# Linear attention and a gated MLP on one core: five chunks of 115 tokens for k^T v, other steps for the extra weight cuts, fetches ahead of stores

## The chip, the core and the metric

The kernel runs on one core of a Trainium2 chip. The metric is the device time of one execution in microseconds; the time before is 957.9 us, the median of five executions (956.86 to 958.39). Engines are called as the profile calls them: PE is TensorE (matmuls; PEld are its weight loads), DVE is VectorE, ACT is ScalarE, POOL is GpSimd, SP is SyncE, which here issues nearly all DMAs.

## What is computed

```python
# q, k, v: float32 [8 batches, 8 heads, 576 tokens, 64]
kv  = einsum('bhsd,bhse->bhde', k, v)          # 64 x 64 per head
o   = einsum('bhsd,bhde->bhse', q, kv)
x   = o / sqrt(mean(o*o, -1) + 1e-6) * g_norm  # 576 x 64 per head
x   = x laid out as (8*576 tokens, 8*64)
h   = x @ w_in                                 # w_in  512 x 2048
g   = h * erf(softplus(h))
out = g @ w_out                                # w_out 2048 x 512
```

The weights come as float64 and are seen by the kernel as pairs of int32, from which it builds float32.

## The kernel before

**Tiling.** Tokens are worked in groups of 512 (`G`), four per partition (`J`). A group T = 0 to 7 is the first 512 tokens of batch T; a ninth group gathers the last 64 tokens of all batches (`x_last`). Heads go in pairs (`NP` = 4 pairs), so that one pair fills 128 partitions. For a pair, `attention` returns six pieces: `products` (k^T v into PSUM, its two 64 x 64 blocks copied into the block-diagonal `bd_kv`, and q transposed), `apply` (q times `bd_kv`), `halve`, `mean`, `norm` (the RMS norm; L330 to L369) and `split`, which writes the three rounded forms of x (`x_forms`, L387 on ACT, then L390 and L393 on DVE).

k^T v sums over the tokens of a batch, 576 of them. The tile of k holds 96 rows (partitions) with six tokens each per head (`KR`, `C`); six matmuls per head, one for each token of a row, add up in PSUM (L281). A pair takes 12 matmuls; each is fp32 and shows as two in the profile. The loads of q, k and v are made in `load_pair`: k and v in one DMA each (L130). A pair's loads are issued two pairs ahead, in `products_and_loads`.

**Stages.** The run has three.

- Stage T=0 (to about 155 us): the weights are loaded raw (`w_raw`, four buffers, L182 and L187), converted on DVE and ACT (`w_split` L197 and L206, `w_join`), and group 0 is multiplied in plain fp32 (`h_ps` L671, `o_ps` L502). SP issues, in order: the first pairs' loads, then raw weights, with the loads of the first two pairs of T=1 between them.
- Stage T=1 (about 150 to 262 us), 16 steps f = 0 to 15: the hidden products go over to three products of rounded forms (L444: `n_ps` two thirds, `m_ps` one third), and the weights are cut into their three parts on the way. `to_cut[f]` lists the tiles cut in step f: `w_upper` makes the first part on ACT (L411), `w_lower` the other two on DVE one step later (L414, L417), and the parts are stored to DRAM (`w_kept`). A tile cut in a buffer of `w_in_p` (four buffers) is stored by one DMA of 768 KB (L484). An extra tile of w_out is cut in place, in columns of `w_in_sb` that are no longer needed, and stored by three DMAs of 256 KB (L480); `places_w` says in which step and in which of three places. In a step, the first two entries of `w_new` get their `w_lower` at the start, a third one after the gates (L697).
- The steady part (262 to 951 us), 28 batches of four hidden blocks, m = 8 to 35, and one more for the last results. A batch does four hidden products (weights from `w_in_parts`), with pieces of the attention of group T+1 between them, and then four results of the batch before (weights from `w_out_parts`), whose sums are added to `e` on DVE (L422 for the first sum, L427 for the second). The order of the instructions on every engine is the order of the program.

**Queues of the steady part.** `places` says behind which of the nine places of a batch (0 ahead of all, 1 to 4 after a hidden product, 5 to 8 after a result) each piece of attention goes; as a rule (0, 2, 3, 5, 6, 8). `FETCH` says which weight parts are fetched at each place; `w_in_p` has four buffers and `w_out_p` seven, and a fetch waits on SP until its buffer is free. In the last batch of a group the four tiles of `e` are stored (L513), each in `result`, that is before the fetch of its place. SP works its queue in order.

These lines carry the steps that the change touches:

```python
for j in range(J):
    result(T2, b2, j, g, w)        # in the last batch of a group: store(T, j, es.pop(j))
    fetch(BATCH + j)
    ...
    pieces(BATCH + 1 + j)
```

Of the kernel before, what the change touches and what calls it, by code (L numbers as in the profile page):

```python
# [39 lines left out]
FP32 = mybir.dt.float32  # L40
# [10 lines left out]
BATCH = 4  # L51
# [9 lines left out]
def kernel(  # L61
# [18 lines left out]
    KC = DM // P  # L80
    FC = DF // P
    NG = B + 1
    KR = 96
    C = S // KR
    assert D == 64 and R == 64 and B == 2 * J and DM == H * D and KC == NP and C * KR == S

    const = ctx.enter_context(tc.tile_pool(name="const", bufs=1))
    kvp = ctx.enter_context(tc.tile_pool(name="kvp", bufs=2))
# [26 lines left out]

    q_last = const.tile([P, 2, 2, D], FP32, name="q_last")

    def load_pair(i):
        T, p = divmod(i, NP)
        if T >= B:  # L120
            return
        pool = early if i in (2, 3) else kvp
        side = nc.scalar if i < 3 else nc.sync
        t = q_sb[T, p] = pool.tile([P, J, 2, D], FP32, name="q_sb", tag="q")
        nc.sync.dma_start(
            out=t, in_=q[T, 2 * p : 2 * p + 2, 0:G, :].rearrange("h (p j) d -> p j h d", j=J)
        )
        for name, got, src in (("k", k_sb, k), ("v", v_sb, v)):
            t = got[T, p] = pool.tile([KR, 2, C, D], FP32, name=f"{name}_sb", tag=name)
            side.dma_start(  # L130
                out=t.rearrange("r h c d -> r h (c d)"),
                in_=src[T, 2 * p : 2 * p + 2].rearrange("h (r c) d -> r h (c d)", c=C),
            )

    def load_last(T, p):
        if T < B:
# [118 lines left out]
    def attention(T, p, pools=None):  # L255

        st = {}

        halves = FIRST <= T < B
        bd = bd_kv[:, (T * NP + p) % 2, :]  # L260

        q_tail, o_tail = slice(P, 2 * P), slice(2 * P, 2 * P + R)

        def bank(name):
            pool, tag = (pools or {}).get(name, (ps_at, "at"))
            return pool.tile([P, G], FP32, name=name, tag=tag)

        def square_tile(name):

            if T == 0:  # L270
                return gate.tile([P, G], FP32, name=name, tag="h")
            return attp.tile([P, G], FP32, name=name, tag="qT")

        def products():

            kv_ps = st["kv"] = bank("kv_ps")
            ks, vs, qs = (x.pop((T, p)) for x in (k_sb, v_sb, q_sb))
            for c in range(C):
                for i in range(2):
                    s = slice(i * D, i * D + D)  # L280
                    nc.tensor.matmul(  # L281
                        kv_ps[s, s],
                        lhsT=ks[:, i, c],
                        rhs=vs[:, i, c],
                        start=(c == 0),
                        stop=(c == C - 1),
                    )
            if p % 2 == 0:
                nc.tensor.transpose(kv_ps[:, q_tail], q_last[:, p // 2], ident)
            if p == NP - 2:  # L290
                for i in range(NP):
                    load_last(T + 1, i)
            st["qT"] = square_tile("qT")
            for i in range(2):
                s = slice(i * D, i * D + D)
                nc.vector.tensor_copy(out=bd[s, s], in_=kv_ps[s, s])
            if p % 2 == 0:
                tails[T] = attp.tile([P, P], FP32, name="qT_last", tag="t")
                nc.vector.tensor_copy(out=tails[T], in_=kv_ps[:, q_tail])
            st["tail"] = tails[T][:, p % 2 * R : p % 2 * R + R]  # L300
            qt_ps = bank("qt_ps")
            for j in range(J):
                nc.tensor.transpose(qt_ps[:, j * P : j * P + P], qs[:, j], ident)  # L303
            nc.scalar.copy(st["qT"], qt_ps)

        def apply():
            qT, o_ps, kv_ps = st["qT"], bank("se_ps"), st.pop("kv")
            nc.tensor.matmul(kv_ps[:, o_tail], lhsT=bd, rhs=st.pop("tail"), start=True, stop=True)
            nc.tensor.matmul(o_ps, lhsT=bd, rhs=qT, start=True, stop=True)  # L309
            nc.vector.tensor_copy(out=x_last[:, p, T * R : T * R + R], in_=kv_ps[:, o_tail])  # L310
            st["o"] = o_ps
            nc.scalar.activation(qT, o_ps, AF.Square)

        def square():
            st["o"], st["qT"] = x_last[:, p, :], square_tile("sq")
            nc.scalar.activation(st["qT"], st["o"], AF.Square)

        def halve():
            sq = st.pop("qT")
            hi = st["hi"] = attp.tile([P, G], FP32R, name="sq_hi", tag="rms_r")  # L320
            lo = st["lo"] = attp.tile([P, G], FP32R, name="sq_lo", tag="sq_lo")
            nc.vector.tensor_copy(out=hi, in_=sq)
            nc.vector.tensor_tensor(out=lo, in0=sq, in1=hi.bitcast(FP32), op=ALU.subtract)

        def mean(table=True):
            ms = st["ms"] = bank("ms_ps")
            if halves:


                nc.tensor.matmul(ms, lhsT=mean_w, rhs=st.pop("hi"), start=True, stop=False)  # L330
                nc.tensor.matmul(ms, lhsT=mean_w, rhs=st.pop("lo"), start=False, stop=True)
                u = square_tile("u")
            else:
                u = st.pop("qT")
                nc.tensor.matmul(ms, lhsT=mean_w.bitcast(FP32), rhs=u, start=True, stop=True)
            if T > 0:
                r = attp.tile([P, G], FP32, name="rms_r", tag="rms_r")
                exp_ln_table()
            else:
                r = gate.tile([P, G], FP32, name="rms_r", tag="s")  # L340
            st["u"], st["r"] = u, r
            nc.scalar.activation(r, ms, AF.Ln, bias=eps_col)  # L342
            nc.scalar.activation(r, r, AF.Exp, scale=-0.5)  # L343
            nc.scalar.activation(u, r, AF.Square)
            if table and (T > 0 or p == NP - 1):
                softplus_table()

        def norm():
            ms, u, r = (st.pop(name) for name in ("ms", "u", "r"))
            nc.vector.scalar_tensor_tensor(  # L350
                out=u, in0=ms, scalar=EPS, in1=u, op0=ALU.add, op1=ALU.mult
            )
            nc.vector.scalar_tensor_tensor(
                out=u, in0=u, scalar=3.0, in1=r, op0=ALU.subtract, op1=ALU.mult
            )
            if T < FIRST:
                if T not in xT:
                    xT[T] = wide.tile([P, KC, G], FP32, name="xT", tag="h")
                x = xT[T][:, p, :]
            else:  # L360
                x = st["x"] = x_new.tile([P, G], FP32, name="x", tag="x")
            nc.vector.scalar_tensor_tensor(
                out=x,
                in0=st.pop("o"),
                scalar=gm_col,
                in1=u,
                op0=ALU.mult,
                op1=ALU.mult,
            )  # L369

        def split():
            if T >= FIRST:
                thirds(st.pop("x"), *(form[:, p] for form in x_forms[T]))

        def products_and_loads():
            products()
            load_pair(T * NP + p + 2)

        if T == 0:
            return products, apply, halve, mean, norm  # L380
        first = (products_and_loads, apply) if T < B else (lambda: None, square)
        return (*first, halve if halves else lambda: None, mean, norm, split)
# [218 lines left out]

    others = [("in", f) for f in range(WHOLE)]
    others += [("out", f) for f in (*range(FC - BATCH, FC), *range(FC - BATCH))]
    places_w = {3: 0, 5: 1, 6: 0, 8: 1, 9: 2, 10: 0}
    to_cut = {f: [] for f in range(FC)}
    for f in range(BATCH * (NB - 1)):
        to_cut[f] = [("in", f + WHOLE), others.pop(0)]
        if f in places_w:
            to_cut[f].append((*others.pop(0), places_w[f]))
    to_cut[FC - BATCH] = [("in", FC - 2), ("in", FC - 1)]  # L610
    assert not others
    hs, ss, plain = {}, {}, {}
    whole = FIRST * FC - BATCH
# [131 lines left out]
    def result(T, b, j, g, w):  # L745
# [12 lines left out]
        else:  # L758
            add_scaled(es[j], ps[0], SHIFT - 1.0)
        add(es[j], ps[1])  # L760
        if b == NB - 1:
            store(T, j, es.pop(j))


    FETCH = ("", "in", "in", "out", "in", "out", "in", "out out")
# [2 lines left out]
    for m in range(first_batch, batches + 1):  # L768
# [15 lines left out]
        if T + 1 == B:  # L784
            places = (0, 0, 0, 5, 6, 7)
            if b == NB - 1:

                places, todo[3] = (0, 0, 0, 4, 5, 6), partial(todo[3], table=False)
        elif T + 2 == B and b == NB - 1:
            places = (0, 2, 3, 5, 6, 7)  # L790

        def pieces(place):
# [34 lines left out]
        for j in range(J):  # L827
            result(T2, b2, j, g, w)
            fetch(BATCH + j)
            if j == 1 and m == batches - 1:  # L830
                cut_lower(h, 0, g_next[0])

# [41 lines left out]
```

## Time and profile before

| | us or share |
|---|---|
| median of five executions | 957.9 |
| profiled execution, its own time | 956.94 |
| its span | 955.1 |
| PE busy | 932.7 (98%) |
| DVE busy | 740.6 (78%) |
| ACT busy | 616.2 (65%) |
| DMA queue q1, share of 16 engines | 75.9% |
| granted clock of PE | 1.0 |

The profile is of one execution; the time that is not in its span, 1.84 us, lies around it. Busy times are sums over instructions. The page also lists the costliest groups of instructions with what they waited for, and the DMA issues with the median time from issue to landing; other views list the waits of an engine, the chain that ended last, the instructions in order of time, and the busy time in windows.

### The profile page before, as it was taken

The page shows a single profiled execution, that of the slowest core. Times are in us where ns is not written, and L with a number is a line of the kernel's source. Part 1 is how long each engine was busy: PE and PEld are TensorE (multiplying, and loading weights), DVE is VectorE, ACT ScalarE, POOL GpSimd, SP SyncE. Part 2 cuts the span into 40 slices and gives each one's busy share as a digit, 9 for nine tenths or more (in the row PEclk, how much of TensorE's full clock was granted, in tenths as well). Part 3 has the DMA queues.
Part 4 walks back from the last instruction along what each step waited for, and adds up shares of the span by engine and source line. Part 5 has one row for each costly group of instructions (what it writes and reads, how often), then busy time and mean ns, then how long its engine had stood idle before and what let it go on. Part 6 is the DMA issues. An engine that isn't in the chain of part 4 may idle for free.

```text
span 955.1 us, 11913 instructions
## 1 busy us (share of the span) xinstructions
PE 932.7 (98%) x4384; PEld 686.3 (72%) x4384; DVE 740.6 (78%) x1054; ACT 616.2 (65%) x825; POOL 2.4 (0%) x10
## 2 busy tenths in 40 slices
PE   6999999999999999999999999999999999999998
PEld 4444445556587887888788878887888787878886
DVE  3979957778577887778888887887777777778667
ACT  3889875677666666666666666666666666665552
POOL 0000000000000000000000000000000000000000
PEclk9999999999999999999999999999999999999999
DMA  9856506799599886998689877988796769767972
GB/s 273 268 162 214 163 1 234 274 342 323 210 360 377 310 301 220 312 380 284 221 280 371 311 286 232 358 310 286 225 364 255 265 222 370 281 261 271 365 277 63
DMA packets 110107, 259.80 MB, mean 272 GB/s; under 512 B 44256, under 2 KB 67808, under 8 KB 110048
## 3 DMA queue, kind: packets, MB, share of 16 engines
q1 hardware_dynamic: 108416, 256.73, 75.9%
q10 hardware_dynamic: 1568, 2.29, 0.8%
q8 instruction: 35, 0.57, 0.2%
q14 instruction: 24, 0.20, 0.1%
q0 software_dynamic: 64, 0.00, 0.0%
HBM read 224.40 MB, written 34.60 MB: 271 GB/s over the span
## 4 chain that ended last, share of the span: by engine, by line
PE 69%; DVE 13%; ACT 12%; issue 3%; DMA 2%; SPq 0%; DVEq 0%
PE n_ps L444 36%; PE m_ps L444 18%; PE o_ps L502 5%; PE h_ps L671 3%; PE se_ps L309 3%; PE kv_ps L281 2%; DVE h L427 2%; ACT L105 1%; PE qt_ps L303 1%; ACT s L818 1%; ACT s L822 1%; DVE e L427 1%; DVE g_forms L390 1%; ACT rms_r L342 1%; ACT rms_r L343 1%
## 5 line engine op out<-in xcount | busy, mean ns | idle before, releaser
L444 PE MATMUL n_ps<-x_forms,w_in_parts 128*128 128x512 f32 x896 | 234.0, 402 | 1.3 <-DVE x_forms L390 1.2
L444 PE MATMUL n_ps<-w_out_parts,g_forms 128*128 128x512 f32 x928 | 231.6, 391 | 0.6 <-DMA w_out_parts<-w_out 0.6
L444 PEld LDWEIGHTS n_ps<-w_out_parts,g_forms 128*128 128x128 f32 x928 | 174.2, 188 | 39.3 <-issue 1.4
L444 PEld LDWEIGHTS n_ps<-x_forms,w_in_parts 128*128 128x128 f32 x896 | 166.7, 188 | 46.3 <-issue 9.6
L818 ACT ACTIVATE s<-h 128x512 f32<-128x512 f32 x112 | 71.0, 634 | 177.9 <-DVE h L427 177.9
L427 DVE TENSOR_TENSOR h<-m_ps,h 128x512 f32<-128x512 f32 x116 | 79.9, 689 | 61.5 <-ACT h L816 43.7
L444 PE MATMUL m_ps<-w_out_parts,g_forms 128*128 128x512 f32 x464 | 124.2, 389 | 0.0
L444 PE MATMUL m_ps<-x_forms,w_in_parts 128*128 128x512 f32 x448 | 120.1, 390 | 0.0
L502 PE MATMUL o_ps<-w_out_sb,h_sb 128*128 128x512 f32 x224 | 100.8, 593 | 0.3 <-DVE h_sb L622 0.3
L444 PEld LDWEIGHTS m_ps<-w_out_parts,g_forms 128*128 128x128 f32 x464 | 87.1, 188 | 18.1
L444 PEld LDWEIGHTS m_ps<-x_forms,w_in_parts 128*128 128x128 f32 x448 | 84.1, 188 | 17.5
L427 DVE TENSOR_TENSOR e<-m_ps,e 128x512 f32<-128x512 f32 x116 | 80.3, 692 | 17.9 <-PE m_ps L444 10.4
L422 DVE SCALAR_TENSOR_TENSOR e<-n_ps,e 128x512 f32<-128x512 f32 x88 | 60.3, 686 | 41.6 <-PE n_ps L444 41.6
L502 PEld LDWEIGHTS o_ps<-w_out_sb,h_sb 128*128 128x128 f32 x224 | 42.3, 190 | 48.9 <-issue 46.7
L393 DVE SCALAR_TENSOR_TENSOR g_forms<-g_forms 128x1024 fp32r<-128x1024 f32 x58 | 71.1, 1226 | 2.0
L390 DVE TENSOR_TENSOR g_forms<-h,g_forms 128x1024 fp32r<-128x1024 f32 x58 | 70.6, 1218 | 1.7 <-ACT g_forms L387 1.4
L816 ACT ACTIVATE h<-n_ps 128x512 f32<-128x512 f32 x112 | 65.6, 586 | 8.2 <-PE se_ps L309 4.3
L387 ACT ACTIVATE g_forms<-h 128x1024 fp32r<-128x1024 f32 x58 | 58.9, 1060 | 12.4 <-PE m_ps L444 9.8
L834 DVE TENSOR_TENSOR h<-h,s 128x1024 f32<-128x1024 f32 x56 | 66.0, 1219 | 0.7 <-ACT s L822 0.7
L671 PE MATMUL h_ps<-xT,w_in_sb 128*128 128x512 f32 x144 | 64.9, 594 | 0.8 <-DVE w_in_sb L230 0.6
L108 ACT ACT_TABLE_LOAD x44 | 56.5, 1283 | 0.7
L822 ACT ACTIVATE s<-s 128x1024 f32<-128x1024 f32 x56 | 56.2, 1052 | 0.3
(98 smaller groups left out, 1021.2 us busy)
## 6 DMA issues: line engine op xcount, KB each, us to landing
w_out_parts<-w_out SPq DMA_DIRECT2D x116, 768.0 KB, 8.0
w_in_parts<-w_in SPq DMA_DIRECT2D x112, 768.0 KB, 6.7
w_in<-w_new SPq DMA_DIRECT2D x16, 768.0 KB, 4.8
k_sb<-in_k_dram SPq DMA_DIRECT2D x29, 288.0 KB, 4.8
v_sb<-in_v_dram SPq DMA_DIRECT2D x29, 288.0 KB, 5.1
q_sb<-in_q_dram SPq DMA_DIRECT2D x32, 256.0 KB, 5.0
w_raw<-in_moe_w_out_dram SPq DMA_DIRECT2D x8, 1024.0 KB, 5.4
out_dram<-e SPq DMA_DIRECT2D x32, 256.0 KB, 3.5
```

What stands on the lines that cost most here:

```text
L387: nc.scalar.activation(high, x, AF.Copy, scale=1.0 + 2.0**-13)
L390: nc.vector.tensor_tensor(out=low, in0=x, in1=high.bitcast(FP32), op=ALU.subtract)
L393: nc.vector.scalar_tensor_tensor(out=both, in0=low.bitcast(FP32), scalar=SHIFT, in1=high.bitcast(FP32), op0=ALU.mult, op1=ALU.add,)
L422: nc.vector.scalar_tensor_tensor(out=out_, in0=ps, scalar=scale, in1=out_, op0=ALU.mult, op1=ALU.add)
L427: nc.vector.tensor_tensor(out=out_, in0=ps, in1=out_, op=ALU.add)
L444: nc.tensor.matmul(ps, lhsT=weights(form, k), rhs=moving(form, k), start=(form == forms[0] and k == 0), stop=(form == forms[-1] and k == 3),)
L502: nc.tensor.matmul(o_ps[j], lhsT=g[:, j * P : j * P + P], rhs=w_out_sb[:, f, :], start=(f == 0), stop=last,)
L671: nc.tensor.matmul(plain[i], lhsT=w_in_sb[:, c, i % FC * P : i % FC * P + P], rhs=xT[T][:, c, :], start=(c == 0), stop=(c == KC - 1),)
L816: nc.scalar.activation(h[:, i], n_ps, AF.Copy, scale=SHIFT - 1.0)
L818: nc.scalar.activation(s[:, i], h[:, i], AF.Softplus)
L822: nc.scalar.activation(part(s, i), part(s, i), AF.Erf)
L834: nc.vector.tensor_tensor(out=part(h, half), in0=part(h, half), in1=part(s, half), op=ALU.mult)
```

## The change

It has four parts.

1. From T=1 on, k and v of a batch are cut into five chunks of 115 tokens, and the one token left over goes into a 116th partition of the first chunk, by a DMA of its own. A pair then takes 10 matmuls, of which the first two have 116 rows. T=0 stays at six chunks of 96.
2. The extra cuts of w_out tiles in stage T=1 go from steps 3, 5, 6, 8, 9 and 10 to steps 4, 5, 8, 9, 12 and 13.
3. In the last batch of a group, the store of a tile of `e` follows the fetch of its place.
4. The last piece (`split`) of a group's last pair goes to place 7 rather than 8; this was so already where T + 2 == B, and now holds for every T except T + 1 == B, which keeps the places of its own.

```diff
-    KR = 96
-    C = S // KR
...
+    def chunks(T):
+
+        return 6 if T == 0 else 5
...
         for name, got, src in (("k", k_sb, k), ("v", v_sb, v)):
-            t = got[T, p] = pool.tile([KR, 2, C, D], FP32, name=f"{name}_sb", tag=name)
+            C = chunks(T)
+            rows, rest = divmod(S, C)
+            assert rest < 2
+            t = got[T, p] = pool.tile([rows + rest, 2, C, D], FP32, name=f"{name}_sb", tag=name)
+            heads = src[T, 2 * p : 2 * p + 2]
             side.dma_start(
-                out=t.rearrange("r h c d -> r h (c d)"),
-                in_=src[T, 2 * p : 2 * p + 2].rearrange("h (r c) d -> r h (c d)", c=C),
-            )
+                out=t[:rows].rearrange("r h c d -> r h (c d)"),
+                in_=heads[:, : S - rest].rearrange("h (r c) d -> r h (c d)", c=C),
+            )
+            if rest:
+                side.dma_start(
+                    out=t[rows:, :, 0], in_=heads[:, S - rest :].rearrange("h r d -> r h d")
+                )
...
+            C = chunks(T)
             for c in range(C):
+                rows = slice(0, S // C + (c < S % C))
                 for i in range(2):
                     s = slice(i * D, i * D + D)
                     nc.tensor.matmul(
                         kv_ps[s, s],
-                        lhsT=ks[:, i, c],
-                        rhs=vs[:, i, c],
+                        lhsT=ks[rows, i, c],
+                        rhs=vs[rows, i, c],
...
-    places_w = {3: 0, 5: 1, 6: 0, 8: 1, 9: 2, 10: 0}
+    places_w = {4: 0, 5: 1, 8: 0, 9: 1, FC - 4: 0, FC - 3: 1}
     to_cut = {f: [] for f in range(FC)}
-    for f in range(BATCH * (NB - 1)):
-        to_cut[f] = [("in", f + WHOLE), others.pop(0)]
+    for f in range(FC):
+        if f < FC - BATCH:
+            to_cut[f] = [("in", f + WHOLE), others.pop(0)]
+        elif f == FC - BATCH:
+            to_cut[f] = [("in", FC - 2), ("in", FC - 1)]
         if f in places_w:
             to_cut[f].append((*others.pop(0), places_w[f]))
-    to_cut[FC - BATCH] = [("in", FC - 2), ("in", FC - 1)]
...
         add(es[j], ps[1])
-        if b == NB - 1:
-            store(T, j, es.pop(j))
...
-        elif T + 2 == B and b == NB - 1:
+        elif b == NB - 1:
             places = (0, 2, 3, 5, 6, 7)
...
             fetch(BATCH + j)
+            if b2 == NB - 1:
+                store(T2, j, es.pop(j))
```

More of the change, by code (lines that the diff above doesn't have):

```diff
@@ L82 @@
     NG = B + 1
-    KR = 96
-    C = S // KR
-    assert D == 64 and R == 64 and B == 2 * J and DM == H * D and KC == NP and C * KR == S
+    assert D == 64 and R == 64 and B == 2 * J and DM == H * D and KC == NP
     const = ctx.enter_context(tc.tile_pool(name="const", bufs=1))
```

## The prediction

> **What bounds the kernel now.** I read the page first, then the waits of TensorE (PE), then the timeline at the places the diff touches, then windows for the DMA share. From the page (busy time, share, instructions; queue: packets, MB, share of 16 DMA engines; issues: count, size, median us to landing):
>
> ```profile
> PE 932.7 (98%) x4384; PEld 686.3 (72%) x4384; DVE 740.6 (78%) x1054; ACT 616.2 (65%) x825; POOL 2.4 (0%) x10
> ...
> DMA packets 110107, 259.80 MB, mean 272 GB/s; under 512 B 44256, under 2 KB 67808, under 8 KB 110048
> ...
> q1 hardware_dynamic: 108416, 256.73, 75.9%
> ...
> w_out_parts<-w_out SPq DMA_DIRECT2D x116, 768.0 KB, 8.0
> w_in_parts<-w_in SPq DMA_DIRECT2D x112, 768.0 KB, 6.7
> ...
> k_sb<-in_k_dram SPq DMA_DIRECT2D x29, 288.0 KB, 4.8
> ```
>
> PE is busy 98% at full clock. Everything else matters only where PE waits, and those waits are few (total, times, longest):
>
> ```profile
> PE kv_ps L281 <- DMA v_sb<-in_v_dram: 7.7, 2, 6.4
> PE kv_ps L308 <- DVE bd_kv L296: 2.2, 2, 1.4
> PE ms_ps L335 <- ACT rms_r L342: 1.3, 1, 1.3
> PE n_ps L444 <- DVE x_forms L390: 1.2, 2, 0.8
> PE se_ps L309 <- ACT qT L304: 1.0, 1, 1.0
> ```
>
> So a removed matmul pays in full, and a late load would cost in full. The timeline of PE shows one pair's k^T v and two starts of hidden products: a group's first batch (461.14) and an ordinary batch (511.21):
>
> ```profile
> 461.14 2.32 PE L444 MATMUL n_ps<-x_forms,w_in_parts 128*128 128x512 f32 x8
> 463.30 1.10 PE L444 MATMUL m_ps<-x_forms,w_in_parts 128*128 128x512 f32 x4
> ...
> 509.84 0.92 PE L281 MATMUL kv_ps<-v_sb,k_sb 96*64 96x64 f32 x24
> 510.69 0.33 PE L289 MATMUL kv_ps<-ident,q_last 128*128 128x128 f32 x1
> ...
> 511.21 2.10 PE L444 MATMUL n_ps<-x_forms,w_in_parts 128*128 128x512 f32 x8
> 513.15 1.07 PE L444 MATMUL m_ps<-x_forms,w_in_parts 128*128 128x512 f32 x4
> ```
>
> Windows (start:end, length, busy PE, PEld, DVE, ACT, POOL, granted clock, DMA share, GB/s) give the load of the DMA engines: a startup stretch, two of stage T=1, one group of the steady part.
>
> ```profile
> 14.00:30.00 16.00, 14.41 (x86) 7.51 (x86) 12.49 (x28) 13.19 (x23) 0.00 (x0) 1.00 1.07 294
> 180.00:190.00 10.00, 9.51 (x29) 5.11 (x28) 9.28 (x16) 4.43 (x8) 0.00 (x0) 1.00 1.04 365
> 190.00:200.00 10.00, 10.00 (x35) 6.23 (x34) 7.88 (x13) 8.48 (x12) 0.00 (x0) 1.00 1.03 391
> 462.00:562.00 100.00, 100.00 (x524) 80.66 (x523) 80.13 (x115) 63.75 (x86) 0.00 (x0) 1.00 0.85 299
> ```
>
> The sum is made against the profiled execution: 956.94 us (span 955.1, 1.84 around it), 0.96 below the median 957.9. Within 0.2% means 956.0 to 959.8.
>
> **k^T v.** From T=1 on a pair issues 10 matmuls for 12; the 24 rows above (two per fp32 matmul) become 20. From 509.84 to 510.69 is 0.85 us for 24, 35.4 ns each; four fewer are 0.142 us. Twenty-eight pairs change; 20 sit in the full steady part, and of the 8 in stages 0 and T=1, where PE idles a little, I count 5. 25 × 0.142 = **-3.5**; ends: -4.0 (all 28) and 0, should a matmul take longer for more rows (35.4 × 115/96 = 42.5; 20 of these are 0.85 again). The nearest row against that: the L308 matmuls, 128 rows and 64 moving columns but twice the stationary columns, at 85 ns, which separates nothing. I take the fixed time: this row is the only one with 64 columns on both sides, and no row shows a duration that grows with the rows.
>
> **The loads of k and v.** This is the risk. A load has 115 rows of 1280 B per head instead of 96 of 1536 B, and a second small DMA brings the last token; 56 more DMAs stand on SP's queue, at 0.4 to 0.7 us of issue each (rows L130), while SP waits 320 us for tiles to free (L577), so issue itself costs nothing; without that cover a batch would wait some 1 us more. But how are rows dealt to the 16 DMA engines? Every DMA in the trace has 64, 96 or 128 rows, all multiples of 16. Of the 44,256 packets under 512 B, 36,864 are q's (32 × 1024 of q_sb and 32 × 128 of q_last); the 7,392 left are 16 × 462, for 460 issued DMAs: as if each ended with one packet on each of 16 engines, equal shares. 115 is 5 × 23. If equal shares stay the rule, 5 engines carry such a load. Bounds: 16 engines (nothing changes) and 1 engine.
>
> The Trainium skill, "DMA: Bandwidth & Descriptors", section "Why a DMA increments its semaphore by 16 and not by 1", states that the engine count is the largest number up to 16 that divides the slowest dimension of both sides, on the lowest-numbered engines: 115 rows would get 5, and a load of two heads by 64 would get 2 for the lone token. This speaks against the change; the trace cannot show it, as all its row counts divide by 16. By it the sum is the one below; with the even spread it would be the first rival's.
>
> I take five, the same five each time (the worse choice). An engine moves 256.73 MB / (0.759 × 955.1 us × 16) = 22.1 GB/s while busy, 391/16 = 24.4 in the fullest window. A load of 294,400 B (k's 288 KB less the last tokens) puts 58.9 KB on each of five, 2.66 us, where 18.4 KB took 0.83: +1.83 per load, **+3.66 per pair** on the hot engines. What that does, by stage:
>
> - *Steady part.* A group has four pairs: the share of 0.85 in a group of 99.4 us becomes (84.5 + 14.6)/99.4 = 1.00 on five engines at 22.1 GB/s; at 24.4 the same bytes (299 × 99.4 / 16 = 1.86 MB, plus 8 × 40.5 KB = 2.18 MB) take 89 us, 0.90. It just fits, more so as five engines alone share less. Cover: w_in parts are issued at 539.10 and used after 561.01, 22 us; w_out parts some 14 us ahead; landings take 8.0 and 6.7 us. A pair's +3.66 fits under that. **0**; the other end is the slower rival's.
> - *Stage T=1.* The chain runs here through the landing of w_out<-w_new (183.12, 7.29 us) into the cut at 190.43. The loads of a pair at 181.22 and 182.01 stand just ahead: +3.66 on hot engines, less two 256 KB stores of step 3's extra, which move a step on (2 × 16 KB / 22.1 = 2 × 0.73): +2.2; step 6's extra cut (0.52 at 191.06) leaves the chain: **+1.6**. Step 3's extra also leaves DVE (176.30 to 177.63, 1.33) just before PE's 1.42 wait for bd_kv at 179.33, and returns one step later ahead of the next cut: -0.9, as far as the chain behind it is not later. Step 12's new extra puts 0.52 on ACT ahead of the qT copy at 237.08, for which PE waits from 237.9: +0.3. The moved stores (3 DMAs each) stand before the w_in_parts of L709, whose use is 20 us off: 0. Together **+1.0**, ends -1.0 (even spread, wait gone) and +3 (landing at the slow rate of window 14:30, 294/1.07/16 = 17.2 GB/s).
> - *Startup.* Two pairs of T=1 are issued from 17.0 to 22.8, ahead of the w_raw at 26.68, needed at DVE's L197 at 37.91; at 5.3 us to landing it has 5.9 us of cover. 2 × 3.66 = 7.3: 1.4 over, of which I take **+0.5** because the backlog drains before the last part queues; ends 0 and +1.5.
>
> **Last piece one place earlier.** In each group the `split` of the last pair (the 0.69 L390 and 0.69 L393 on DVE) now goes ahead of result j=3's two adds. Today it is late at four group starts: from the first n_ps to its m_ps the timeline shows 2.62 us (360.84 to 363.46), 2.16 (461.14 to 463.30), 2.15 (561.01) and 2.15 (660.88), against 1.94 in an ordinary batch (511.21 to 513.15). The excess goes: **-1.3** = 0.68 + 0.22 + 0.21 + 0.21; ends 0 and -1.5. What becomes late are the e adds of j=3, by 1.4 us; behind them wait a PSUM bank that is reused three products later (9 us) and the store: covered. Next at a group start comes the weight tile, which landed long before.
>
> **Parts ahead of stores.** In a group's last batch each fetch passes its store on SP. PE waits 0.6 for w_out_parts once (at 795.35, first product of a results batch): **-0.6**, ends 0 and -0.7. Now the last store waits behind fetches that wait for buffers; e is rewritten only with the next group's first result, some 20 us later: 0. Behind the store stand the next pair's q, k, v, used a batch (25 us) later.
>
> Sum: -3.5 + 0 + 1.0 + 0.5 - 1.3 - 0.6 = **-3.9**: 953.0 on the profiled execution, **954.0** on the median.
>
> **The rivals.**
> 1. *Rows spread evenly over 16 engines.* Then T=1 is -0.6, startup 0: 952. For it: nothing in the trace; against: 115 has no equal shares by 16.
> 2. *Early stages eat the gain.* Both upper ends, 1.0→3 and 0.5→1.5, give 957; with loads also late at the se_ps wait of 209.7 (another 3) 960. For it: DMA share 1.03 to 1.07 there, the fullest of the run. Against: PE's waits in that stage are short.
> 3. *A 115-row matmul takes longer.* The first term is 0: 957.5. For: nothing separates it; against: stated above.
> 4. *Slower: five engines fall behind in the steady part.* 471 KB per group on a hot engine at the rate of the startup window, 17.2 GB/s, is 27.4 us; the other 1.71 MB at 22.1 is 77.4: 104.8 in 99.4. Each of five groups slips 5.4, 27 in all; 14 of cover absorb part: 967, without cover 981. Decides below 471 / (99.4 - 77.4) = 21.4 GB/s for these rows. For: 22.1 is close. Against: each batch leaves SP 10 us blocked (L577 at 548.74), room to catch up, and the fullest window reached 24.4.
>
> **How the numbers follow.** Chances: the forecast 0.50 (own range 952 to 956), rival 1 0.12, rival 2 0.20, rival 3 0.08, rival 4 0.10. Faster: forecast and rival 1, less a twentieth: 0.60. Same: most of rivals 2 and 3: 0.25. Slower: rival 4 and the tail of 2: 0.15. The range, 950.5 to 960.5, takes in rivals 1 to 3 and leaves rival 4 out.
>
> **What would show it.** Matmul records L281 x20 a pair with the same 35 ns spacing; k and v to landing rising from about 5 us to 7 or more while q stays; group starts at 1.94; no PE wait for k_sb, v_sb or parts after 262; the w_out<-w_new landing before 190 later by 1 to 2. It is wrong if L281 spacing grows to 42, if PE shows waits for w_in_parts or w_out_parts in each group (rival 4), or if stage T=1 ends over 2 us later.

## The result and the profile after

The changed kernel takes 959.54 us, the median of 24 executions (957.86 to 962.46). The kernel before, run beside it, has a median of 957.52. The ratio is 1.0020, 95% interval 1.0015 to 1.0026: slower by about 1.9 us, where 3.9 us faster were forecast. The time lies inside the stated range, on the wrong side of no change. Its profiled execution took 959.01 us (span 957.2).

The page of the changed kernel (busy times; packets; the queue):

```profile
PE 929.7 (97%) x4272; PEld 683.2 (71%) x4272; DVE 741.1 (77%) x1054; ACT 616.4 (64%) x825; POOL 2.4 (0%) x10
...
DMA packets 111843, 259.78 MB, mean 271 GB/s; under 512 B 43865, under 2 KB 69545, under 8 KB 111785
...
q1 hardware_dynamic: 110152, 256.73, 76.1%
```

PE has 112 instructions and 3.0 us of busy time less (932.7 before), and yet the end is 2.1 us later: 5.1 us of waiting are new. The waits of PE and, in the second fence, of ACT name the largest of them, that for h, which the kernel before doesn't have:

```profile
PE n_ps L456 <- ACT h L828: 3.1, 1, 3.1
PE se_ps L321 <- ACT qT L316: 2.1, 2, 1.1
PE n_ps L456 <- ACT h_sb L700: 1.5, 2, 0.9
...
PE kv_ps L320 <- DVE bd_kv L308: 1.0, 1, 1.0
```

```profile
ACT h L828 <- DMA out_dram<-e: 9.2, 1, 9.2
```

So once in the run ACT can't write h for 9.2 us until a store of e has landed, and PE stands behind it for 3.1. The timelines put it in place. Kernel before, SP, PE and ACT, where the first group of the steady part is stored:

```profile
285.73 0.38 SPq L577 DMA_DIRECT2D w_in_parts<-w_in  x1
286.70 0.34 SPq L513 DMA_DIRECT2D out_dram<-e  x1
287.09 0.96 SPq L577 DMA_DIRECT2D w_out_parts<-w_out  x2
...
285.40 2.09 PE L444 MATMUL n_ps<-x_forms,w_in_parts 128*128 128x512 f32 x8
...
292.50 0.60 ACT L816 ACTIVATE h<-n_ps 128x512 f32<-128x512 f32 x1 [4.32 <-PE se_ps L309]
```

The changed kernel, the same places on SP, ACT and PE:

```profile
286.23 0.34 SPq L525 DMA_DIRECT2D out_dram<-e  x1
286.62 0.90 SPq L589 DMA_DIRECT2D w_out_parts<-w_out  x2
288.14 0.34 SPq L525 DMA_DIRECT2D out_dram<-e  x1
...
298.18 0.60 ACT L828 ACTIVATE h<-n_ps 128x512 f32<-128x512 f32 x1 [9.18 <-DMA out_dram<-e]
...
298.83 1.42 PE L456 MATMUL n_ps<-x_forms,w_in_parts 128*128 128x512 f32 x5 [3.07 <-ACT h L828]
```

Two fetches of 768 KB now stand ahead of the last store, and the store lands so late that h starts at 298.18 instead of 292.50 (1.06 of this lag was there already at the start of the steady part). The late h costs PE another 0.9 at 305: 0.67 and 0.23 before the two ms_ps products, whose squares come late from DVE. Why h needs a store of e: the four results of this group (T2 = 1) are not in the buffer that the later groups use. `sums` takes their tile from `wide` with tag "h", the two buffers that the tiles h of the steady batches rotate through (`sums(*((acc, "e") if T2 < FIRST - 1 else (wide, "h")))`). The h of the second steady batch is that buffer. Already in the kernel before, ACT idled 4.32 us at this place. The row names se_ps of PE, but the n_ps that is copied was complete at 287.49 (issued 285.40, 2.09 us), so what is left is the buffer (a run below names the store in this row); PE just did not feel it.

Where the time went, by four marks of each profile: the first softplus of T=1 (L688 before), the first of the steady part, the first of its second batch and the last one (all L818 before). Each column is the time from the mark before:

| us | to T=1 | T=1 | first steady batch | rest |
|---|---|---|---|---|
| before | 143.43 | 122.63 | 27.81 | 635.81 |
| changed | 143.48 | 123.63 | 32.43 | 632.31 |
| difference | +0.05 | +1.00 | +4.62 | -3.50 |

The gain is there, 3.5 us in the steady part. The loss sits in one batch that the sum had set to zero.

### The profile page after: what moved, and what is told of

Read it like the earlier page. It is cut to its first block, busy times and chain, and to the rows that moved or that the text cites. A ratio compares the mean times of both kernels' runs of the same rounds, so it can differ in the third digit from the quotient of the medians.

```text
span 957.2 us, 11752 instructions
## 1 busy us (share of the span) xinstructions
PE 929.7 (97%) x4272; PEld 683.2 (71%) x4272; DVE 741.1 (77%) x1054; ACT 616.4 (64%) x825; POOL 2.4 (0%) x10
## 2 busy tenths in 40 slices
DMA packets 111843, 259.78 MB, mean 271 GB/s; under 512 B 43865, under 2 KB 69545, under 8 KB 111785
## 4 chain that ended last, share of the span: by engine, by line
PE 76%; ACT 8%; DVE 7%; DMA 6%; SPq 1%; issue 1%; DVEq 0%
PE n_ps L456 41%; PE m_ps L456 20%; PE o_ps L514 5%; PE h_ps L685 3%; PE se_ps L321 2%; PE kv_ps L293 2%; DMA v_sb<-in_v_dram 1%; DMA w_out_parts<-w_out 1%; PE qt_ps L315 1%; DMA w_raw<-in_moe_w_in_dram 1%; DMA w_in<-w_new 1%; ACT L103 1%; DMA w_out<-w_new 1%; ACT w_e L215 1%; ACT s_sb L720 1%
```

## The experiments

Two theories for the 4.6 us stood against each other. S: the order on SP's queue delays the store. H: the loads of k and v, on five DMA engines, delay it whatever the order. Beside that, each part's own worth was open. All times of before in this section are medians of runs on the same chip at the same time (957.09 to 957.28).

**Stores first again.** The change without its third part:

```diff
         add(es[j], ps[1])
+        if b == NB - 1:
+            store(T, j, es.pop(j))
...
             fetch(BATCH + j)
-            if b2 == NB - 1:
-                store(T2, j, es.pop(j))
```

> The change without its third part: each store stands ahead of the fetch of its place again. Theory S (the store of the first steady group's last tile waits behind fetches, and that tile's buffer is the next h): the delay of 4.6 us between the softplus at 266 us and the one at 294 us goes, PE's wait of 3.07 for the copy of h goes, the time is 959.5 - 4.6 + 0.6 = 955.5. Theory H (the store lands late because k and v load five DMA engines, whatever its place in the queue): the wait stays within 1 us of 3, and the time stays at 959 or above.

Measured: 956.07 us, ratio 0.9992 (0.9983 to 1.0000). The first steady batch takes 28.01 us, PE's wait for the copy of h is gone. The loads are the same as in the changed kernel, so with these loads it is the order that decides: S.

**Fetch first alone.** The kernel before with that diff the other way round.

> The kernel before with the third part alone, so all k and v loads have 96 rows. Theory S: the same wait for the copy of h in the first steady group, 957.5 + 3 to 5 less 0.6 saved later, 960 to 962. Theory H: no wait, 957.0 to 957.5.

Measured: 959.63 us, ratio 1.0036 (1.0023 to 1.0049), with all k and v loads as before: 0.4 under the range that S gave, 2 above that of H. In its profile the first steady batch takes 29.74 us, 1.93 more than before, and the rest 635.65 for 635.81. (The profiled execution took 958.42, 1.2 below the median.) So the third part loses time even with 96-row loads, by 2.4 us between the medians. The saving of 0.6 for later groups is not in the sum of the rest, 0.16 at most. PE's waits show why, first of the kernel before, then of this one:

```profile
PE n_ps L444 <- DMA w_out_parts<-w_out: 0.6, 1, 0.6
```

```profile
PE n_ps L444 <- ACT x_forms L387: 0.7, 1, 0.7
```

The wait for w_out_parts at 795.35 did go, as the prediction had it; but at the start of the last group PE then waits 0.66 (at 854.10) for x_forms from ACT, where it didn't before. What was gained is waited away there.

**Chunks of 115 alone.** The first part of the change and nothing else.

> The kernel before with the first part alone: five chunks of 115 tokens and one more. If the recorded terms of the prediction hold: matmuls -3.0 (25 pairs by the 0.12 us that the pair at 285.07 shows), five hot engines in stage T=1 +2 to +3 (the extras of steps 3 and 6 stay where they were, so both stand on the path of the landing at 190), startup 0 to 0.5: 956.5 to 957.5. If the hot engines cost nothing it is 954.5. If they also delay the store of the first steady group, 959 or more.

Measured: 959.75 us, ratio 1.0029 (1.0018 to 1.0040). Stage T=1 takes 127.06 us, +4.4, more than expected; the first steady batch 29.55, +1.7 with the stores first; the rest 634.26, only -1.55. (The profiled execution took 961.34, 1.6 above the median, so the +4.4 and +1.7 may be too large.) So H has a share after all in the first steady batch, though with the change's other parts and the stores first it was 0.2, and the first part by itself loses.

**Extras alone.** The second part and nothing else.

```diff
-    places_w = {3: 0, 5: 1, 6: 0, 8: 1, 9: 2, 10: 0}
+    places_w = {4: 0, 5: 1, 8: 0, 9: 1, FC - 4: 0, FC - 3: 1}
```

> The kernel before with the second part alone: extras of w_out in steps 4, 5, 8, 9, 12 and 13. By the prediction's terms: 0.6 us of ACT leaves the chain at 191, two 256 KB stores leave the queue ahead of the landing at 190 (-1.5), the wait of 1.42 for bd_kv goes, +0.3 at 237: 955.5 to 957.0. A rival: what it saves before 190 is given back by the extras' stores that now stand behind the landing, 957.5.

Measured: 955.41 us, ratio 0.9982 (0.9973 to 0.9991). Stage T=1 takes 120.42 us, -2.2: a gain, 0.1 past the good end of the expectation.

**Place 7 alone.**

```diff
-        elif T + 2 == B and b == NB - 1:
+        elif b == NB - 1:
```

> The kernel before with the fourth part alone: the last piece at place 7 in every group. By the prediction: the excess at four group starts goes, -1.3, 956.2. A rival: the adds of e that it moves behind itself hold something else up, 957.5 or more.

Measured: 955.46 us, ratio 0.9982 (0.9973 to 0.9991); the rest of the steady part 634.44, -1.37, as forecast; the median is 0.7 below the 956.2 expected.

**Five engines or the number of DMAs?** The kernel before with its matmuls untouched; only each load from T=1 on is cut in two, once at row 95 and once at row 80. 95 is 5 × 19; 80 and 16 divide by 16.

```diff
-            side.dma_start(
-                out=t.rearrange("r h c d -> r h (c d)"),
-                in_=src[T, 2 * p : 2 * p + 2].rearrange("h (r c) d -> r h (c d)", c=C),
-            )
+            to = t.rearrange("r h c d -> r h (c d)")
+            of = src[T, 2 * p : 2 * p + 2].rearrange("h (r c) d -> r h (c d)", c=C)
+            for rows in (slice(0, KR),) if T == 0 else (slice(0, 95), slice(95, KR)):
+                side.dma_start(out=to[rows], in_=of[rows])
```

> The kernel before, matmuls unchanged, with each k and v load from T=1 on cut in two DMAs of 95 rows and 1 row. Theory F (95 is 5 x 19, so five engines carry the load, and that is what the first part costs): the first part alone gave +2.5 while its matmuls save 18 to 20 pairs x 0.12 = 2.2 to 2.4, so the loads cost some +4.8 and this takes 961 to 963. Rival N (the number of DMAs on the queue, 56 more, or the shape of rows costs it): the same time as the cut in 80 and 16 rows.

> The control: the same with 80 rows and 16 rows, both multiples of 16, as many DMAs and bytes as with 95 and 1. Theory F: 957.0 to 958.5, nothing but 56 issues on a queue that waits anyway. Rival N: 961 to 963.

Measured: 95 + 1 takes 962.19 us, ratio 1.0057 (1.0043 to 1.0070); 80 + 16 takes 956.72, ratio 0.9997 (0.9989 to 1.0006), 0.3 under what was expected of it. The same bytes in the same number of DMAs on the same queue differ by 5.5 us through the row counts alone. In stage T=1 it is 126.53 against 122.61 us, in the first steady batch 28.55 against 27.53, and nothing in the rest (635.86 and 635.79).

The page also shows on how many engines a DMA lies. Packet counts of 95 + 1, then of 80 + 16:

```profile
DMA packets 109603, 259.80 MB, mean 271 GB/s; under 512 B 43752, under 2 KB 67304, under 8 KB 109544
```

```profile
DMA packets 111003, 259.80 MB, mean 272 GB/s; under 512 B 45152, under 2 KB 68704, under 8 KB 110944
```

Take off q's 36,864 packets of 256 B, and 16 for each of the 406 DMAs that all versions share (462 less the 56 that were cut): 6,496. From 43,752 there remain 392 for 56 pairs of DMAs, 7 a pair: 5 and 2. From 45,152 there remain 1,792, 32 a pair: 16 and 16. The changed kernel gives 43,865 - 36,864 - 6,496 - 112 (its last tokens are two 256 B rows each) = 393, again 7 a pair. This is what the rule of the Trainium skill, "DMA: Bandwidth & Descriptors", section "Why a DMA increments its semaphore by 16 and not by 1", says of 115 rows and of two: five engines and two.

The chain shows where it costs in stage T=1, first of the kernel with 95 + 1, then of its control with 80 + 16 (7.29 us and 190.43 in the kernel before):

```profile
184.91 9.06 DMA w_out<-w_new
193.96 0.02 issue
193.98 0.64 ACT w_new L411
```

```profile
184.24 6.25 DMA w_out<-w_new
190.50 0.02 issue
190.52 0.63 ACT w_new L411
```

The cut behind the landing starts 3.46 us later with 95 + 1, close to the +3.66 a pair that the prediction had.

**Chunks of 128 and 64.** The first part with rows that spread over 16 engines: four chunks of 128 tokens and one of 64.

```diff
-            rows, rest = divmod(S, C)
+            rows, per = (S // C, C) if T == 0 else (P, C - 1)
...
-                rows = slice(0, S // C + (c < S % C))
+                rows = slice(0, S // C if T == 0 else R if c == C - 1 else P)
```

> The first part in another shape: from T=1 on four chunks of 128 tokens and one of 64 (rows 0 to 63), also 10 matmuls a pair and two DMAs a load, of 128 and of 64 rows. Theory F: the matmul gain stays and the loss goes, 957.4 - 2.2 - 0.4 (8 pairs before 262 us) = 955. Rival N: 959 or more, like the chunks of 115.

Measured: 957.54 us, ratio 1.0007 (0.9998 to 1.0016). The expected 955 did not come. The loads were no longer late (stage T=1 122.40 us), but the rest of the steady part took 636.23, longer than before. Its PE timeline, a pair of 20 matmuls and, from two narrower windows, the last six and the last four of them:

```profile
509.97 0.95 PE L292 MATMUL kv_ps<-v_sb,k_sb 128*64 128x64 f32 x20
510.85 0.33 PE L300 MATMUL kv_ps<-ident,q_last 128*128 128x128 f32 x1
```

```profile
510.43 0.49 PE L292 MATMUL kv_ps<-v_sb,k_sb 128*64 128x64 f32 x6
```

```profile
510.59 0.33 PE L292 MATMUL kv_ps<-v_sb,k_sb 64*64 64x64 f32 x4
```

Twenty matmuls (as the profile counts them) take 0.88 us here (509.97 to 510.85), more than the 24 of before (0.85). From the last two with 128 rows (510.43) to the first with 64 (510.59) it is 0.16 us, where two otherwise take 0.06 (the last ten start at 510.31, the last six at 510.43). That is how the next shape came about.

**Chunks of 128 and 96.** Three chunks of 128 tokens and two of 96, so that every DMA has 128 or 96 rows and no matmul 64.

```diff
+    def parts(T):
+        return ((KR, 6),) if T == 0 else ((P, 3), (KR, 2))
...
+            for rows, per in parts(T):
+                side.dma_start(
+                    out=t[:rows, :, c0 : c0 + per].rearrange("r h c d -> r h (c d)"),
+                    in_=heads[:, at : at + rows * per].rearrange("h (r c) d -> r h (c d)", c=per),
+                )
+                c0, at = c0 + per, at + rows * per
...
+                rows = slice(0, P if T > 0 and c < 3 else KR)
```

> The first part in a third shape: from T=1 on three chunks of 128 tokens and two of 96; all DMAs have 128 or 96 rows and no matmul has 64. With chunks of 128 and one of 64 the pair took 0.88 us for 20 matmuls (509.97 to 510.85), no less than the 0.85 of 24; the records show 59 ns for each two matmuls of 128 rows, but some 150 more around the two pairs of matmuls with 64 rows. Theory W (the change to a 64-row weight tile costs that): here the pair takes 0.73, 20 x 0.12 are saved, 957.4 - 2.6 = 954.8. Rival (128 rows are themselves slower, or a change of rows between chunks costs): 957 or more.

Measured: 954.82 us, ratio 0.9973 (0.9963 to 0.9984). PE's timeline:

```profile
508.91 0.80 PE L294 MATMUL kv_ps<-v_sb,k_sb 128*64 128x64 f32 x20
509.64 0.33 PE L302 MATMUL kv_ps<-ident,q_last 128*128 128x128 f32 x1
```

0.73 us a pair, as with 115 rows (285.07 to 285.80 in the changed kernel). So 128 rows are no slower than 96; what costs 0.15 is the chunk of 64 rows among longer ones.

**Stores first for the first group alone.** The change, with the order of before only where T2 is 1.

```diff
+            if T2 == 1 and b2 == NB - 1:
+                store(T2, j, es.pop(j))
             fetch(BATCH + j)
-            if b2 == NB - 1:
+            if T2 != 1 and b2 == NB - 1:
                 store(T2, j, es.pop(j))
```

> The change with its third part undone for the first steady group alone (T2 = 1), where e lies in a buffer of h. Theory S: 2.7 to 4.6 less than the change, 955 to 957, and 0 to 0.6 below the change with all stores first (956.1). If the other groups' stores behind their fetches cost too: 957.5 or more.

Measured: 955.16 us, ratio 0.9982 (0.9973 to 0.9991), against 1.0020 of the change: 0.0038 × 957 = 3.6 us for four stores in one group. The first steady batch takes 28.30 us for 32.43. ACT's row for h (at 292.50 before and 298.18 after the change) now names the store, with the stores first:

```profile
293.59 0.60 ACT L828 ACTIVATE h<-n_ps 128x512 f32<-128x512 f32 x1 [5.04 <-DMA out_dram<-e]
```

**What the findings make together.** Chunks of 128 and 96, the extras and place 7; once with all stores first, once with the third part in all groups but the first.

> Chunks of 128 and 96, the second and the fourth part of the change, all stores ahead of the fetches. If the terms add: 957.4 - 2.4 (matmuls) - 1.8 (extras) - 1.5 (place 7) = 951.7. If the matmul gain is used up elsewhere: 954.

> The same with the third part in all groups but the first. If fetching ahead of stores helps the later groups by the 0.6 of the prediction: 951.1; if not, 951.7.

Measured: 951.37 us, ratio 0.9941 (0.9929 to 0.9954), and 951.43, ratio 0.9943 (0.9930 to 0.9955). Both medians are 5.7 us below the kernel before, and the order of stores in the later groups makes no difference.

## Why the prediction was wrong, step by step

- **Parts ahead of stores: the step that failed.** The sum had -0.6. The sentence "e is rewritten only with the next group's first result, some 20 us later: 0" is true of every group but the first, whose e lies in a buffer of h. There the price is +3.6 (the change against the same with only that group's stores put back; 4.1 between the first steady batches of the profiles). It turns the sign: without it the change gains 1.9 us (955.16 for 957.09), which is still only half of the 3.9 forecast. The saving that was expected, 0.6 at one wait for w_out_parts, does come there and goes again in a new wait for x_forms at the last group start: 0.16 less in the rest with the third part alone, and none between the last two kernels.
- **The loads on five engines: right in kind and nearly in size.** Shown by 95 + 1 against 80 + 16. Stage T=1 was summed to +1.0 and came out at +1.00 (+1.1 and +1.2 in the two runs with stores put back). The landing ahead of the cut at 190 ends 1.64 later (192.07 for 190.43), as forecast. The pieces of that sum: the loads were put at +3.66 a pair and gave +3.9 in that stage (126.53 against 122.61, the two cuts); the extras were put at -2.7 (-1.5 for two stores, -0.6 on ACT, -0.9 on DVE, +0.3) and gave -2.2 alone. These two make +1.7, not +1.0, so that the sum came out to the hundredth is in part luck: how the pieces overlap was not measured. For the startup +0.5 was taken, and the first softplus of T=1 comes 0.05 later, although the raw load that stood at 26.68 was issued at 31.57. That settles nothing: three profiles with the same startup (the change and the two runs with stores put back) have this mark at 142.94 to 144.80. The steady part proper was put at 0, which 635.86 against 635.79 confirms; rival 4 is out. Only the first steady batch, where the DMA engines are nearly full (share 0.89 to 1.05 from 270 to 300 before), was missed: +1.0 with 95 + 1, +1.7 with chunks of 115.
- **k^T v: right in kind, a third of it missing.** The sum had -3.5; chunks of 128 and 96 alone, where no load is late, gain 2.3 by the medians. Each pair was to save 0.142 us and saves 0.12 (0.85 to 0.73): if four cost 0.12, 24 cost 0.72, and dividing the 0.85 by 24 spread over them the other 0.13, which a pair costs whatever their number. And of the 25 pairs counted, 18 lie in the rest; nothing of the others is seen in stage T=1 (122.58 with those chunks, 122.62 before). Rows don't matter between 96 and 128, so rival 3 is out as it was put, though 64 rows do. And one pair of each group stands just ahead of the group's start, where PE waits for x_forms: without the fourth part its saving becomes wait. With chunks of 128 and 96 alone, the first n_ps of such a group takes 2.26 us (460.24 to 462.50) for 2.16 before; the four starts lengthen by 0.1 to 0.2 each. That is why the rest gives only -1.54 with the chunks alone where 18 × 0.12 is 2.2, and -3.5 in the change, which has both (-1.37 for place 7 alone).
- **Place 7:** -1.3 forecast, -1.37 in the profile.
- **The rivals.** Rival 2 gave the right time (957 to 960) by the wrong mechanism: the early stages cost what the forecast had taken for them. Rival 1 is out: by the packet counts five engines carry the loads. What ended on the slow side was none of those written down, a store whose buffer has another user.

What stays open: by itself the third part costs 1.9 us in the first steady batch of its profile and 2.4 by the medians; five engines alone cost 1.0 to 1.7 there; the same loads in the change with the stores first cost 0.2; the change, with both, 4.6. So the parts don't add up there. It may depend on how full the DMA engines are when the stores are issued, but no run here varied that by itself. Nor was it tried why the changed kernel's executions spread over 4.6 us (957.86 to 962.46) where those of before spread over 2.1.

## What to carry to other kernels

Before an instruction that frees a buffer is moved back on a queue, list every tile that ever takes that buffer, the first and last round of a loop above all: the pool and tag decide it, not the tile's name. Count the rows of a DMA before a tile is cut to fill partitions better: 115 rows went to five engines, 96 and 128 to sixteen, and 576 tokens can be had in five chunks as 3 × 128 + 2 × 96. A sum of small terms needs each edit's worst place, not its usual one: here one term, priced at the usual place, took back more than all the others together gave. And a wait that goes must be followed to the end: the 0.6 came back at the next group start.

## What the hardware showed unexpectedly

- A matmul chunk of 64 rows after chunks of 128 costs about 0.15 us a pair (0.88 us for 20 matmuls, against 0.73 with 128 and 96 rows), more than the 0.12 that four matmuls fewer save.
- Where loads lie on five engines, the page lists no median of issue to landing, not even for the 768 KB fetches: so with the changed kernel, the chunks of 115 alone and 95 + 1, while 80 + 16 has them (7.5 us for w_out_parts). So whether the landings of k and v rose to 7 us, as the prediction said, can't be read there. The small packets then still tell the engines, as above.
